# Transposing q and k between the scores of two pairs, and weight conversion behind the first norm, in a fused attention and feed-forward kernel

## The chip, the cores and the metric

The kernel runs on one core of a Trainium2 chip. The metric is the device time of one execution in microseconds (us). All runs quoted here are of the state "fast" (granted TensorE clock 0.996 to 0.999 on average), so they can be compared with each other.

Engine names in the profile: PE is TensorE's matmuls, PEld its weight loads, DVE is VectorE, ACT is ScalarE, POOL is GpSimd, SP is SyncE, which issues most transfers; SPq is its queue. A PSUM bank is one of the buffers that the program's matmuls write to; a tag is the program's name for a group of them.

## The reference, cut to what matters

```python
# attention: q, k, v of shape (8, 12, 448, 64)
q_n, k_n = rmsnorm(q, g_q), rmsnorm(k, g_k)
scores = matmul(q_n, k_n^T) / sqrt(64)
attn = exp(scores - max) / sum(exp(scores - max))
out = matmul(attn, v)
# x: (8 * 448, 768), then a feed-forward block
xn = x / sqrt(mean(x*x) + 1e-6) * rms_g
y = (silu(xn @ w_gate) * (xn @ w_val)) @ w_out      # weights arrive as float64
```

Heads are taken in pairs: 8 batches of 6 pairs make 48. The weights are float64 and must be made float32 on the chip. That is the "conversion": 72 pieces, each in a "turn" that also moves on the pieces before it.

## The kernel before: the parts that the change and the argument touch

One function writes the program, and the traces show VectorE and ScalarE taking their instructions in the order in which that function issues them. In the trace before, ScalarE's L532, which VectorE's copy L533 waits for, ended at 106.71 us (106.10 + 0.61), and the copy ran at 108.79, behind an L748 that was issued ahead of it and started at 107.48. `pe(fn)` issues one piece of TensorE work, and `after(n, fn)` issues something n such pieces later. Two names are alike: `turn(g, i)` transposes q or k of pair g, and `turns(n)` issues n turns of the conversion. One turn of the conversion touches every engine but TensorE:

```python
def convert():                       # turn n; loads, splits, joins and adds of different pieces
    n = turn_of["n"]
    ...
    nc.gpsimd.tensor_tensor(data(key), top, lo, ALU.add)       # L785, GpSimd: piece n-5
    join(...)    # L746, L747, L748, VectorE: piece n-4
    split(...)   # L740, L741, ScalarE: piece n-3
    load_raw()   # L727, SyncE: piece n, into one of 7 raw buffers
    keep(...)    # L773, SyncE: piece n-7 to memory
```

The transposes of q and k. Outside the first pairs (`todo` not empty) both use tag m, which has one bank:

```python
def turn(g, i):                       # i = 0: q, i = 1: k
    ps = (ps_m if todo else ps_f).tile(..., tag="m" if todo else "f")
    for t in range(3):
        nc.tensor.transpose(ps[:, ...], src[:, ...], ident)                    # L527
    if i == 0:
        nc.tensor.transpose(ps[:, 384:], rest, ident)                          # L531
        nc.scalar.activation(qT, ps[:, 0:448], Copy, scale=gqk)                # L532
        nc.vector.tensor_copy(kT[:, LAST], ps[:, 448:])                        # L533
    else:
        nc.vector.tensor_copy(kT[:, FULL], ps[:, FULL])                        # L535
```

The rest of a pair is `score` (L545, six matmuls on four banks of tag s, each followed by an exp on ScalarE, L549), `rests` (L575, L581, L586; the exp is L590), `values` (L597), `sums` (L610, then reciprocal L614 or L618 and multiply L625 on VectorE). L581 starts a product in the bank of tag m and therefore waits for L625 of the pair before (in the trace before, one L625 ends at 43.21 us and the L581 behind it starts at 43.36).

The loop, for the pairs that run alone (1 to 6), for pair 7 with the first norm, and for the stage after, where projections of the feed-forward (L1121) fill the gaps:

```python
for g in range(NG + 1):
    ...
    if g <= NPAIR:                                   # NPAIR = 6
        pe(lambda: score(g, (0,)))
        squares(g + 2, 0); squares(g + 2, 1)
        if g > 1:
            pe(lambda: turn(g + 1, 0)); some_rests(g); pe(lambda: turn(g + 1, 1))
        pe(lambda: rests(g))
        pe(lambda: values(g - 1))
        ...
        turns(1 if g == 1 else 3 if g < NPAIR else 0)      # conversion
        pe(lambda: sums(g - 1))
        pe(lambda: score(g, (1, 2)))
        turns(2 if g == 1 else 3 if g == NPAIR else 0)     # conversion
        continue
    pe(lambda: (rests(g), score(g, (0,)) if g < NG else None))
    if g == NPAIR + 1:
        pe(lambda: rms_x(0))                         # L645, L647, L649
    pe(lambda: values(g - 1))
    if g == NPAIR + 1:
        pe(lambda: score(g, (1,))); pe(lambda: norm_x(0)); pe(lambda: score(g, (2,)))   # L657, L663
    pe(lambda: sums(g - 1))
    if g == NPAIR + 1:
        begin(0, 15)                                 # from here projections lie in todo
    ...
    fill(); squares(...); pe(lambda: turn(g + 1, 0)); some_rests(g); fill()
    pe(lambda: turn(g + 1, 1)); fill()               # every item of a fill is followed by one turn of conversion
```

## Time and profile before

| | before |
|---|---|
| median of 3 runs | 1598.26 us (1598.19 to 1600.19) |
| TensorE busy, of a span of 1596.4 us | 1571.4 us |
| VectorE busy / GpSimd busy | 872.9 / 658.6 us |
| first value product (L597) starts at | 18.98 us |
| feed-forward (L1121) starts at | 97.74 us |
| value products of pair 7 start at | 118.61 us |

First TensorE at the start of the feed-forward (start in us, duration, operation; a wait would stand at the end of a line in brackets):

```profile
104.61 0.49 PE L527 MATMUL tr<-ident,qn 128*128 128x128 f32 x3
104.94 0.27 PE L531 MATMUL tr<-ident,rest 128*128 128x128 f32 x1
105.05 4.68 PE L1121 MATMUL ff<-x,w 128*128 128x448 f32 x12
109.56 0.49 PE L527 MATMUL tr<-ident,qk 128*128 128x128 f32 x3
109.89 6.93 PE L1121 MATMUL ff<-x,w 128*128 128x448 f32 x18
```

And VectorE over the same time:

```profile
101.03 0.62 DVE L625 TENSOR_TENSOR x<-av,rd 128x448 f32<-128x448 f32 x1
101.58 0.35 DVE L746 TENSOR_SCALAR xs<-xs 128x384 f32<-128x384 f32 x1
...
108.79 0.21 DVE L533 COPY kT<-tr 128x64 f32<-128x64 f32 x1
```

The q transposes of pair 8 end near 105.1. Their bank is emptied only when L533 ends at 108.79 + 0.21 = 109.00, because nine steps of three conversion turns (and one step of the first projections, L1131) stand ahead of that copy. The k transposes want the same bank at 109.56. The slack is 0.56 us. No wait is seen, so nothing in the list of waits points here.

### The profile page before, as it was taken

To read this page: it belongs to the slowest core of one execution; us is meant where nothing else is said; L and a number is where in the kernel's file an instruction comes from. 1 tells how busy PE (TensorE), PEld (TensorE's weight loads), DVE (VectorE), ACT (ScalarE), POOL (GpSimd) and SP (SyncE) were. 2 spreads that over 40 slices of the span, in tenths; PEclk is the share of its full clock that TensorE was granted. 3 is DMA by queue.
4 is the path that set the end of the run, shared out by engine and by line. 5 is a ranking of instruction groups with operands and counts; after the bars stand their busy time and mean duration, and the time that the engine had idled before them with its cause. 6 is when DMAs were issued, how large, how long until landed. Compare 5 with 4: busy or idle time off the path is not lost.

```text
span 1596.4 us, 21562 instructions
## 1 busy us (share of the span) xinstructions
PE 1571.4 (98%) x7286; PEld 1113.4 (70%) x7286; DVE 872.9 (55%) x1556; ACT 470.4 (29%) x940; POOL 658.6 (41%) x712
## 2 busy tenths in 40 slices
PE   8999999999999999999999999999999999999998
PEld 4344445687756887578865788667885688859974
DVE  6889898578823556236562354625563355613531
ACT  6745563232222222222232222323322222101010
POOL 6867877465334443343434443443542342000000
PEclk9999999999999999999999999999999999999999
DMA  7648574957746554465545655584554544457651
GB/s 211 205 152 257 162 251 125 289 184 246 247 140 206 151 160 118 143 204 150 157 119 144 205 154 146 152 264 134 159 144 123 179 139 138 120 172 217 175 151 55
DMA packets 261996, 273.28 MB, mean 171 GB/s; under 512 B 78836, under 2 KB 258804, under 8 KB 261876
## 3 DMA queue, kind: packets, MB, share of 16 engines
q1 hardware_dynamic: 260948, 271.61, 56.7%
q8 instruction: 60, 0.98, 0.3%
q14 instruction: 60, 0.49, 0.1%
q10 hardware_dynamic: 800, 0.20, 0.1%
q0 software_dynamic: 128, 0.00, 0.0%
HBM read 232.40 MB, written 39.32 MB: 170 GB/s over the span
## 4 chain that ended last, share of the span: by engine, by line
PE 79%; DVE 7%; issue 1%; POOL 0%; DMA 0%; ACT 0%; SPq 0%; DVEq 0%; POOLq 0%
PE ff L902 40%; PE ff L1093 22%; PE sc L545 6%; PE av L597 5%; PE sc L575 2%; PE den L610 2%; PE tr L527 1%; DVE top L747 1%; DVE top L748 1%; DVE top L746 1%; PE ff L1003 1%; DVE rd L618 1%; DVE h L925 0%; DVE h L924 0%; DVE raw L984 0%
## 5 line engine op out<-in xcount | busy, mean ns | idle before, releaser
L902 PE MATMUL ff<-x,w 128*128 128x224 f32 x1878 | 381.5, 354 | 3.7 <-DVE h L925 2.6
L902 PEld LDWEIGHTS ff<-x,w 128*128 128x128 f32 x1878 | 351.3, 190 | 19.2 <-issue 11.1
L555 POOL TENSOR_TENSOR es<-e 128x448 f32<-128x448 f32 x82 | 91.6, 1137 | 492.8 <-ACT e L549 492.8
L902 PE MATMUL ff<-xs,w 128*128 128x224 f32 x1374 | 281.4, 353 | 2.9 <-DVE w L858 2.9
L902 PEld LDWEIGHTS ff<-xs,w 128*128 128x128 f32 x1374 | 258.1, 190 | 6.3 <-issue 6.0
L562 POOL TENSOR_TENSOR es<-es,e 64x448 f32<-64x448 f32 (+1 forms) x164 | 191.7, 1179 | 6.3
L618 DVE RECIPROCAL rd<-rd 128x448 f32<-128x448 f32 x41 | 121.0, 2952 | 110.8 <-ACT rd L617 110.8
L549 ACT ACTIVATE e<-sc,rs 128x448 f32<-128x448 f32 x288 | 161.6, 635 | 50.4 <-PE sc L545 48.0
L1093 PE MATMUL ff<-w,h 128*128 128x384 f32 x498 | 167.8, 487 | 0.6 <-ACT p L1072 0.6
L1093 PE MATMUL ff<-w,raw 128*128 128x384 f32 x468 | 159.5, 487 | 0.3 <-DVE y L1065 0.3
L545 PE MATMUL sc<-qT,kT 64*128 64x448 f32 x576 | 138.0, 572 | 1.9 <-ACT e L549 0.7
L1093 PEld LDWEIGHTS ff<-w,h 128*128 128x128 f32 x498 | 93.5, 190 | 64.5 <-issue 1.3
L1093 PEld LDWEIGHTS ff<-w,raw 128*128 128x128 f32 x468 | 87.6, 190 | 60.9 <-issue 2.6
L597 PE MATMUL av<-e,vt 128*64 128x448 f32 x576 | 118.8, 548 | 0.0
L506 POOL TENSOR_TENSOR rs<-ms,mhalf 128x12 f32<-128x12 f32 (+1 forms) x50 | 114.4, 2288 | 4.2
L1121 PE MATMUL ff<-x,w 128*128 128x448 f32 x288 | 111.8, 541 | 0.0
L545 PEld LDWEIGHTS sc<-qT,kT 64*128 64x128 f32 x576 | 53.9, 185 | 82.4 <-issue 68.5
L914 DVE TENSOR_TENSOR cc<-ff,u 128x448 f32<-128x448 f32 x84 | 52.4, 624 | 91.6 <-PE ff L902 91.4
L597 PEld LDWEIGHTS av<-e,vt 128*64 128x64 f32 x576 | 37.1, 136 | 75.6 <-issue 75.6
L1121 PEld LDWEIGHTS ff<-x,w 128*128 128x128 f32 x288 | 53.3, 190 | 50.8 <-issue 49.0
L631 POOL TENSOR_TENSOR ss<-ss,rd 128x448 f32<-128x448 f32 x40 | 46.5, 1163 | 82.9 <-ACT rd L630 82.9
L914 DVE TENSOR_TENSOR u<-ff,p 128x448 f32<-128x448 f32 x42 | 26.1, 622 | 96.8 <-PE ff L902 96.8
(132 smaller groups left out, 1855.8 us busy)
## 6 DMA issues: line engine op xcount, KB each, us to landing
w<-kept SPq DMA_DIRECT2D x511, 192.0 KB, 2.7
w<-kept_o SPq DMA_DIRECT2D x296, 192.0 KB, 2.7
kept<-w SPq DMA_DIRECT2D x89, 192.0 KB, 3.8
qk<-in_q_dram SPq DMA_DIRECT2D x48, 192.0 KB, 2.9
qk<-in_k_dram SPq DMA_DIRECT2D x96, 96.0 KB, 3.3
vt<-in_v_dram SPq DMA_DIRECT2D x48, 192.0 KB, 2.5
raw<-in_moe_w_gate_dram SPq DMA_DIRECT2D x24, 384.0 KB, 4.5
raw<-in_moe_w_val_dram SPq DMA_DIRECT2D x24, 384.0 KB, 4.6
```

The source lines that it names most:

```text
L506: nc.gpsimd.tensor_tensor(st["rs", g][:, cols], ms, mhalf[:, cols], ALU.pow)
L545: nc.tensor.matmul(ps[:, 0:S], lhsT=kT[r, c * 128:(c + 1) * 128], rhs=qT[r, :], start=True, stop=True)
L549: nc.scalar.activation(e, ps[:, 0:S], ACT.Exp, scale=rs[:, n:n + 1])
L555: nc.gpsimd.tensor_tensor(es, st["e", g, 0, j], st["e", g, 1, j], ALU.add)
L562: nc.gpsimd.tensor_tensor(es[r], es[r], e[r], ALU.add)
L597: nc.tensor.matmul(av[own(j), 0:S], lhsT=vt[:, j, c], rhs=st["e", g, c, j], start=False, stop=(c == NK - 1), skip_group_check=True)
L618: nc.vector.reciprocal(rd, rd)
L631: after(1 if soon else 4, lambda: (nc.gpsimd.tensor_tensor(ss, ss, rd, ALU.add), st.update({("summed", b): hp})))
L902: nc.tensor.matmul(bank[:, w * HT:(w + 1) * HT], lhsT=wt[:, c * 128:(c + 1) * 128], rhs=x[:, c, :], start=onto is None and w == c == 0, st ...
L914: nc.vector.tensor_tensor(add[name], ps[:, 0:S], add[other], ALU.add)
L1093: nc.tensor.matmul(ps, lhsT=left_o(b, which, LEFT_O[name], c), rhs=data(("wo", b, name, c)), start=first and c == 0, stop=c == NFP - 1, sk ...
L1121: nc.tensor.matmul(bank[w][:, 0:S], lhsT=data(key)[:, c * 128:(c + 1) * 128], rhs=st["x", 0, half][:, c, :], start=half == c == 0, stop=ha ...
```

## The change

Its intent: in the pairs that run alone, TensorE's six scores in a row stall on banks that ScalarE has still to free (0.55 us of each row, by the prediction's estimate from 3.21 us for twelve matmuls, 1.74 for eight and up to 0.95 for four), so the transposes are put between them. In pair 7 a score fills the wait for a bank. And three conversion turns, which stood ahead of the first norm, are moved behind it.

```diff
         if g <= NPAIR:
+            if g > 1:
+                pe(lambda: turn(g + 1, 0))
+                pe(lambda: turn(g + 1, 1))
             pe(lambda: score(g, (0,)))
             squares(g + 2, 0)
             squares(g + 2, 1)
             if g > 1:
-                pe(lambda: turn(g + 1, 0))
                 some_rests(g)
-                pe(lambda: turn(g + 1, 1))
             pe(lambda: rests(g))
 ...
             pe(lambda: score(g, (1, 2)))
-            turns(2 if g == 1 else 3 if g == NPAIR else 0)
+            turns(2 if g == 1 else 0)
 ...
-        pe(lambda: (rests(g), score(g, (0,)) if g < NG else None))
         if g == NPAIR + 1:
+            pe(lambda: score(g, (0,)))
+            pe(lambda: rests(g))
             pe(lambda: rms_x(0))
+        else:
+            pe(lambda: (rests(g), score(g, (0,)) if g < NG else None))
 ...
         if g == NPAIR + 1:
             begin(0, 15)
+            turns(3)
```

## The prediction

> **What bounds the kernel now.** I read the page first, then the table of busy time by stretch, TensorE's timeline of the first 100 us, VectorE's and GpSimd's beside it, and last the chain that ended last. From the page:
>
> ```profile
> span 1596.4 us, 21562 instructions
> PE 1571.4 (98%) x7286; PEld 1113.4 (70%) x7286; DVE 872.9 (55%) x1556; ACT 470.4 (29%) x940; POOL 658.6 (41%) x712
> ...
> PE 79%; DVE 7%; issue 1%; POOL 0%; DMA 0%; ACT 0%; SPq 0%; DVEq 0%; POOLq 0%
> ```
>
> TensorE is busy all but 25 us (1596.4 - 1571.4), yet the chain runs 7% of the span through VectorE. The two meet early: the change only touches pairs 2 to 7, the attention that runs alone before the first feed-forward work. By stretch (us; PE, PEld, DVE, ACT, POOL):
>
> ```profile
> 26.00:36.00 10.00, 10.00 (x55) 4.15 (x55) 9.79 (x15) 8.84 (x19) 6.30 (x10) 1.00 0.58 153
> 36.00:46.00 10.00, 8.29 (x41) 3.27 (x39) 9.71 (x19) 7.95 (x17) 8.35 (x9) 1.00 0.77 233
> ...
> 76.00:86.00 10.00, 8.81 (x50) 2.91 (x44) 5.37 (x7) 4.42 (x10) 4.66 (x5) 1.00 0.71 225
> 86.00:96.00 10.00, 8.97 (x48) 3.71 (x50) 8.01 (x13) 5.79 (x12) 7.92 (x8) 1.00 0.55 152
> ...
> 200.00:250.00 50.00, 48.75 (x172) 24.25 (x169) 47.76 (x69) 28.37 (x59) 40.28 (x38) 1.00 0.70 224
> ```
>
> See that VectorE has 0.2 to 0.3 us free in ten while TensorE idles 1.7 at 36 to 46, and that VectorE is again 96% busy at 200 to 250. TensorE's timeline (start, us; at the end of a line, idle time and what ended it):
>
> ```profile
> 36.56 3.28 PE L545 MATMUL sc<-qT,kT 64*128 64x448 f32 x12
> 39.77 0.55 PE L527 MATMUL tr<-ident,qn 128*128 128x128 f32 x3
> ...
> 43.36 0.97 PE L581 MATMUL av<-e,vr 64*64 64x448 f32 x4 [1.71 <-DVE row L1231]
> ...
> 82.02 1.77 PE L545 MATMUL sc<-qT,kT 64*128 64x448 f32 x8
> 83.76 0.97 PE L575 MATMUL sc<-qT,kT 64*64 64x448 f32 x4
> 85.92 0.97 PE L581 MATMUL av<-e,vr 64*64 64x448 f32 x4 [1.19 <-issue]
> ...
> 93.86 0.60 PE L657 MATMUL rb<-ident,rs 112*128 112x112 f32 x4 [1.03 <-POOL rs L649]
> ```
>
> The releasers named are not the real ones at 43.36 and 85.92. The value product needs the only bank of tag "m", which the multiply L625 of the pair before must free; VectorE's own rows say when:
>
> ```profile
> 39.61 2.95 DVE L614 RECIPROCAL rd<-den 128x448 f32<-128x448 f32 x1
> 42.59 0.62 DVE L625 TENSOR_TENSOR x<-av,rd 128x448 f32<-128x448 f32 x1
> ...
> 94.49 3.64 DVE L663 SCALAR_TENSOR_TENSOR x<-x,rg,rb 128x448 f32<-128x448 f32 x6 [1.79 <-PE rb L657]
> 98.05 2.95 DVE L614 RECIPROCAL rd<-den 128x448 f32<-128x448 f32 x1
> ```
>
> 42.59 + 0.62 = 43.21, then the matmul at 43.36. Likewise L625 ends at 85.8 ahead of 85.92. Last, the chain in order of time: from 198 us it is one row of VectorE conversion steps (L746 to L748) up to the last converted weights, which TensorE takes at 279.31.
>
> ```profile
> 277.32 1.95 POOL w L785 x2
> 279.26 0.04 issue
> 279.31 6.07 PE ff L1003 x18
> ```
>
> [...] at 36 to 43 us VectorE finishes nine conversion steps before the reciprocal. So reordering one engine's work moves everything behind it. [...] L746 takes 0.35 us at 85.74 and 1.31 at 86.99, with GpSimd's 1.51 us add and its weight adds beside it. [...] Here L533 waits for ScalarE's L532 on the same bank (59.8 us in total, 32 times).
>
> **The change part by part.** No instruction is added or removed; the comparison of the instruction streams shows only moves.
>
> (1) In pairs 2 to 6 the eight transposes move ahead of the first scores. Today six score matmuls come in a row and need banks that ScalarE has yet to free: 12 issues take 39.77 - 36.56 = 3.21 us. Eight take 83.76 - 82.02 = 1.74 and four unhindered about 0.86 to 0.95 (97.17 to 98.12), so about 0.55 us of each row is a stall hidden in "busy". The transposes (40.68 - 39.77 = 0.91 us) now cover it. At face value 5 x 0.55 = 2.8 us. But I followed the queues by hand with these durations, and the loop through VectorE closes again. L625 of a pair frees the bank; then ScalarE's square (0.5), and now two exps (1.0) and a square (0.5) stand behind it; then VectorE's two sums (1.0), three conversions (3 x 1.27 = 3.8, somewhat more with GpSimd), reciprocal and multiply (3.6): 10.4 to 11.1 us. Today the mean pair takes (82.02 - 26.11) / 5 = 11.18. So of the 2.8 us only about 0.5 survives: TensorE comes early and waits for L625. A second check eats the rest: q of pair 4 is normed by GpSimd only at 39.2 us, and the transposes would be ready at about 37.7.
>
> (2) Pair 7: its first score now stands before the wait for L625 of pair 5. Idle 1.2 us is filled with 0.95 us of matmul.
>
> (3) The three conversion turns of pair 6 leave the queues ahead of the norm. Today their nine VectorE steps and three GpSimd adds delay the sum of squares (1.51 instead of 1.14 us) and L647, which waits until 92.55. Without them rms follows the add: by hand L647 at 88, root 1.0 us, so the 1.03 us wait at 93.86 goes. Together TensorE begins the feed-forward at about 95.0 instead of 97.74: 0.5 + 0.95 + 1.03 + about 0.2 = 2.7 us earlier.
>
> (4) The price: the nine steps run after the norm and pair 6's reciprocal. VectorE's norm would end at about 95.3, reciprocal and multiply at 98.9, and 3.8 to 6 us of conversion bring it to 102.7 to 105, where before it stood at the same point at 101.58 (98.05 + 2.95 + 0.62). So VectorE, and with it GpSimd's adds, starts the next stage 1 to 3.5 us later, while TensorE starts 2.7 earlier.
>
> (5) From there to 279 us both matter. Today VectorE is held by TensorE at two reciprocals (0.61 at 122.48, 0.51 at 148.27) and GpSimd twice, through ScalarE's tanh, before its sum (0.82 and 0.79); an earlier TensorE gives these 2.7 us back. +1 to +3.5 minus 2.7 is -1.7 to +0.8 at about 200 us. After that the conversion chain has no slack, so its end moves by just that, and TensorE, 2.7 us early, waits at the last output products for it. After 279 TensorE is the bound and the shift stays. The middle of -1.7 to +0.8 is -0.5; I shade it to -1.3, because GpSimd's stretching in (4) is the least sure term and the nine steps may run at their 3.8 us. 1598.26 - 1.3 = about 1597.
>
> **Rivals.** *The whole gain arrives*: TensorE is 98% busy, and if it paces the stage 97 to 279, the 2.7 us (or 5 with all of (1)) reach the end: 1593 to 1595.5. For it: conversion's ScalarE steps stand behind tanhs that wait for TensorE (29.2 us in 12 waits at 96 to 290). Against: VectorE has under 3 us free in 200 to 277. *The conversion slips*: if the nine late steps collide with GpSimd's sums of exps, the ring of four buffers (ScalarE waits 31.9 us for GpSimd's adds there) carries 3 us to the end: 1600 to 1601.5. *The early transposes wait for the norm of q*: pairs gain nothing or lose a few tenths each, TensorE starts at about 96 and the end is 1598 to 1599. A new stall at the single "m" bank in the stage after, where the copy L533 already holds TensorE 0.83 us at 241.20, would look the same.
>
> **Range and chances.** All terms are a few us of 1598, 0.2% each; 2% is 32 us and no path reaches it. The runs before spread by 2.0 us. Prediction 1597.0, range 1594.0 to 1600.0; faster by over 2%: 0.01, within 2%: 0.98, slower: 0.01.
>
> **What would show it.** (1) the row of six scores becomes two rows of 1.7 and 0.9 us with a visible idle before L581 in pairs 3 to 6, ended by L625; pair period 11.0 to 11.2. (2), (3) no wait before the norm's transposes, the first L1121 at 94 to 96 us. (4) VectorE's multiply of pair 6 ends near 99, and the ninth step at 103 to 105. (5) idle of TensorE between 200 and 280 grows from about 2 us to 4 or so, and the first output product after the last conversion starts at 277 to 280. It would be wrong if that product starts by 276, which means TensorE paced the stage, or if the pair period falls below 10.7.

## The result, and the profile after

The changed kernel took 1607.05 us (median of 4; 1606.74 to 1608.88), the kernel before 1598.22 us (median of 4; 1597.96 to 1600.19). The ratio is 1.0055, with a 95% interval of 1.0038 to 1.0072. Ratios here are the mean time of one kernel's fast runs over that of the other's in the same rounds, so not quite the ratio of the medians. The change made the kernel slower by some 9 us: inside 2%, but outside the predicted range and with the wrong sign.

The page after, span, engines and chain:

```profile
span 1605.0 us, 21557 instructions
PE 1572.9 (98%) x7286; PEld 1113.5 (69%) x7286; DVE 873.0 (54%) x1556; ACT 471.0 (29%) x940; POOL 659.5 (41%) x712
...
PE 80%; DVE 5%; POOL 0%; DMA 0%; issue 0%; SPq 0%; ACT 0%; DVEq 0%; POOLq 0%
```

Busy times hardly move. TensorE's idle time grows from 25.0 to 32.1 us (1605.0 - 1572.9), and its busy time by 1.5 us. TensorE's waits name the idle time (total, times, longest):

```profile
PE tr L527 <- DVE kT L533: 7.7, 2, 6.9
...
PE tr L527 <- POOL qn L511: 1.9, 1, 1.9
```

One wait is 6.9 us long. In TensorE's timeline, to be held against the one of before:

```profile
104.44 4.68 PE L1121 MATMUL ff<-x,w 128*128 128x448 f32 x12
116.01 0.90 PE L527 MATMUL tr<-ident,qk 128*128 128x128 f32 x3 [6.90 <-DVE kT L533]
116.71 8.74 PE L1121 MATMUL ff<-x,w 128*128 128x448 f32 x18
```

VectorE after, over the same time:

```profile
100.42 0.62 DVE L625 TENSOR_TENSOR x<-av,rd 128x448 f32<-128x448 f32 x1
100.96 0.35 DVE L746 TENSOR_SCALAR top<-top 128x384 f32<-128x384 f32 x1
...
106.13 0.35 DVE L746 TENSOR_SCALAR xs<-xs 128x384 f32<-128x384 f32 x1
...
108.91 1.28 DVE L746 TENSOR_SCALAR xs<-xs 128x384 f32<-128x384 f32 x1
...
115.75 0.21 DVE L533 COPY kT<-tr 128x64 f32<-128x64 f32 x1
```

The three moved turns occupy VectorE from 100.96 to 106.13, which is 5.2 us. The turns behind them are now stretched too (1.28 us for an L746 that took 0.35). L533 comes at 115.75 instead of 108.79, 7.0 us later: 4.55 because the steps ahead of it start later (106.13 instead of 101.58), 2.41 because these same steps take 9.62 us instead of 7.21. GpSimd was adding beside them (L555, 2.66 us from 107.31); no run separates this stretching from the later place. The slack was 0.56, so TensorE waits.

The wait has a second cost. The table of stretches (busy of PE, PEld, DVE, ACT, POOL; the first number after those is the granted TensorE clock) shows it:

```profile
109.00:116.00 7.00, 0.11 (x1) 0.00 (x0) 6.86 (x9) 0.99 (x2) 5.98 (x6) 0.82 0.77 221
116.00:120.00 4.00, 3.99 (x8) 2.33 (x9) 3.86 (x9) 0.00 (x0) 3.76 (x4) 0.50 0.30 108
```

While TensorE idles, its granted clock falls to 0.50, and the 18 projection matmuls behind the wait take 8.74 us instead of 6.93. By a finer cut of the same table the clock is 1.00 up to about 113.5, 4.4 us into the wait, and at 0.50 until about 120.3, 4.3 us after work began again.

Because the run-up, the stretch ahead of the first value product, varies (last section), I count every kernel's times from its first value product. The 6.90 us of wait, 1.81 us of slow projections and 0.37 us of slow transposes (starts 0.70 instead of 0.33 us apart) are 9.08 us. The value products of pair 7 come 108.38 us after the first instead of 99.63, 8.75 us later, although the feed-forward had started 0.49 us earlier (78.27 instead of 78.76). So 9.24 us were lost between, and 9.08 of them have a name. From there on the distance stays between 8.7 and 8.8 us to the end.

The early pairs did not gain either. TensorE's waits in pairs 3 to 5 after:

```profile
39.80 0.55 PE L527 MATMUL tr<-ident,qn 128*128 128x128 f32 x3 [1.85 <-POOL qn L511]
...
54.64 0.97 PE L581 MATMUL av<-e,vr 64*64 64x448 f32 x4 [0.74 <-DVE kT L533]
...
66.30 0.97 PE L581 MATMUL av<-e,vr 64*64 64x448 f32 x4 [0.80 <-DVE kT L533]
```

Twelve scores in a row took 3.28 us; eight now take 1.77 us and the four behind the transposes 1.02, so most of the stall among them is gone. But the time comes back as a wait for the norm of q and as waits at L581, where the real releaser is again L625 (in pair 4 it ends at 54.49, and L581 starts at 54.64). The reason is the loop that the prediction named, on ScalarE in pair 4, first before, then after:

```profile
50.73 3.26 ACT L549 ACTIVATE e<-sc,rs 128x448 f32<-128x448 f32 x6 [2.61 <-PE sc L545]
53.84 0.97 ACT L484 ACTIVATE sq<-qk 128x384 f32<-128x384 f32 x2
...
55.19 0.61 ACT L630 ACTIVATE rd<-x 128x448 f32<-128x448 f32 x1
```

```profile
54.59 0.58 ACT L630 ACTIVATE rd<-x 128x448 f32<-128x448 f32 x1 [1.44 <-DVE x L625]
55.07 1.14 ACT L549 ACTIVATE e<-sc,rs 128x448 f32<-128x448 f32 x2
56.10 0.93 ACT L484 ACTIVATE sq<-qk 128x384 f32<-128x384 f32 x2
```

The square L630 waits for L625, and the exps and squares that used to run ahead of it now stand behind it. VectorE's sums, and so the next reciprocal, come late. From one pair's value products to the next, from pair 2 up to pair 5, it now takes 11.59, 11.66 and 10.66 us; before, it took 10.45, 11.45 and 10.45. At pair 5 the changed kernel is 1.37 us behind (59.75 against 58.38 after the first value product).

### The profile page after: what moved, and what is told of

The parts are those of the page before. It is cut to its first block, busy times and chain, and to the rows that moved or that the text cites.

```text
span 1605.0 us, 21557 instructions
## 1 busy us (share of the span) xinstructions
PE 1572.9 (98%) x7286; PEld 1113.5 (69%) x7286; DVE 873.0 (54%) x1556; ACT 471.0 (29%) x940; POOL 659.5 (41%) x712
## 4 chain that ended last, share of the span: by engine, by line
PE 80%; DVE 5%; POOL 0%; DMA 0%; issue 0%; SPq 0%; ACT 0%; DVEq 0%; POOLq 0%
PE ff L902 40%; PE ff L1093 22%; PE sc L545 6%; PE av L597 5%; PE sc L575 2%; PE den L610 2%; PE tr L527 1%; PE ff L1003 1%; DVE top L747 1%; DVE top L748 1%; DVE top L746 0%; PE ff L1121 0%; DVE rd L618 0%; DVE h L925 0%; DVE h L924 0%
## 5 line engine op out<-in xcount | busy, mean ns | idle before, releaser
L555 POOL TENSOR_TENSOR es<-e 128x448 f32<-128x448 f32 x82 | 92.1, 1144 | 493.7 <-ACT e L549 493.7
L785 POOL TENSOR_TENSOR w<-top,raw 128x384 int32<-128x384 int32 x63 | 67.0, 1078 | 39.2 <-DVE top L748 25.9
```

Source lines behind the costliest of these rows:

```text
L555: nc.gpsimd.tensor_tensor(es, st["e", g, 0, j], st["e", g, 1, j], ALU.add)
L785: nc.gpsimd.tensor_tensor(data(key).bitcast(I32), top, lo, ALU.add)
```

## The experiments

Theory A: the three turns stand ahead of L533 in VectorE's queue, the one bank of tag m is freed late, TensorE waits and its clock falls. Rival B: the transposes between the scores push the queues late. Rival C: the order of score, last rows and rms in pair 7 does it. Rival D came later: it does not matter where the turns stand, the stage has no room for three more.

All medians of the changed kernels are of 4 runs (5 for the one with the turns behind k in the kernel before, and for the last); those of the kernel before are of 4, 7 or 9 runs on the same chip. "Distance" is counted in one trace of each kernel: the start of the value products of pair 14 after the first ones, minus the 296.63 us of the kernel before.

| kernel | median us | kernel before, same chip | ratio (95%) | feed-forward starts after first value product | distance, us |
|---|---|---|---|---|---|
| before | 1598.2 | | | 78.76 | 0 |
| changed | 1607.05 | 1598.22 | 1.0055 (1.0038 to 1.0072) | 78.27 | +8.74 |
| changed, turns back at pair 6 | 1600.62 | 1598.32 | 1.0017 (1.0000 to 1.0034) | 80.15 | +1.44 |
| before, turns moved alone | 1607.16 | 1598.32 | 1.0053 (1.0036 to 1.0070) | 77.67 | +8.93 |
| before, pairs alone | 1601.25 | 1598.32 | 1.0016 (0.9999 to 1.0033) | 80.13 | +1.41 |
| before, pair 7's order alone | 1599.60 | 1598.32 | 1.0007 (0.9990 to 1.0024) | 78.79 | +0.08 |
| changed, own bank for k of pair 8 | 1605.96 | 1598.25 | 1.0044 (1.0029 to 1.0060) | 78.25 | +6.19 |
| changed, idle matmuls in the wait | 1606.40 | 1598.25 | 1.0051 (1.0035 to 1.0066) | 78.19 | +6.56 |
| changed, turns behind k of pair 8 | 1604.52 | 1598.25 | 1.0037 (1.0022 to 1.0053) | 78.27 | +6.46 |
| before, pair 7's order, turns behind k of pair 8 | 1603.87 | 1598.25 | 1.0033 (1.0019 to 1.0047) | 76.87 | +3.94 |
| changed, turns left to the last burst | 1602.66 | 1599.26 | 1.0024 (1.0009 to 1.0040) | 78.22 | +3.78 |
| before, pair 7's order, one turn each in pairs 9 to 11 | 1603.07 | 1599.26 | 1.0022 (1.0007 to 1.0037) | 76.87 | +4.91 |
| before, pair 7's order, turns ahead of pair 5's sums | 1596.81 | 1599.26 | 0.9990 (0.9977 to 1.0004) | 77.36 | -1.42 |

All gave correct results. The count can be checked: 1598.19 us (the profiled run of the kernel before), plus the distance, plus what the first value product comes later than 18.98 us, gives the time of every other profiled run to 0.15 us (to 0.4 in the one with a turn each in pairs 9 to 11). So the distances tell the kernels apart where the medians, mixed from runs of both run-ups, do not.

### One part undone, each part alone

**The turns back at pair 6.**

```diff
-            turns(2 if g == 1 else 0)
+            turns(2 if g == 1 else 3 if g == NPAIR else 0)
 ...
             begin(0, 15)
-            turns(3)
```

> The changed kernel, but pair 6's three conversion turns stand ahead of the norm again, as before the change. Theory A (the nine VectorE steps that now stand ahead of L533, the copy that frees the one bank of tag m, make the k transposes of pair 8 wait; the granted clock then falls): no wait of over 1 us at those transposes, L533 at 108 to 109 us, the end at 1597 to 1599 us, so all of the 8.6 us come back. Rival B (the transposes between the scores push the queues late): the end stays at 1604 to 1607 us. Rival C (the order of score, last rows and rms in pair 7): stays there too.

The wait is gone and 7.3 of the 8.74 us come back (+1.44). The median lies 1.6 us above the expected range, and L533 came at 110.2 rather than at 108 to 109. I had still taken the pairs for neutral, and they cost 1.4. (Two of its four runs, at 1601.3 and 1601.6, lie 1.4 us or more above the other two, as runs with the slow run-up of the last section do.) Theory A gained on B and C, but not for the whole sum.

**The turns moved alone**, in the kernel before.

```diff
-            turns(2 if g == 1 else 3 if g == NPAIR else 0)
+            turns(2 if g == 1 else 0)
 ...
             begin(0, 15)
+            turns(3)
```

> The kernel before with only the three turns moved behind the norm. Theory A: the same wait, 6 to 8 us, at the k transposes of pair 8 on L533, a granted clock of about 0.8 in the 20 us around it, and the end at 1605 to 1608 us. Rivals B and C: within 2 us of the kernel before, 1596 to 1600 us.

As theory A says:

```profile
117.02 0.90 PE L527 MATMUL tr<-ident,qk 128*128 128x128 f32 x3 [6.92 <-DVE kT L533]
```

The granted clock is 0.74 between 110 and 130 us, and the median 1607.16 us. This part alone makes the whole loss. It also brings what it was meant for: without the turns ahead of it the norm's transposes no longer wait 1.03 us, and the feed-forward starts 1.09 us earlier.

**The pairs alone**: the transposes of pairs 3 to 7 between the scores, in the kernel before (the diff's first hunk).

> The kernel before with only the transposes of pairs 3 to 7 moved between the scores. Theory A: no long wait at the k transposes of pair 8; the pair period stays at 11.0 to 11.5 us because L625 closes the loop, and the end lies within 1.5 us of the kernel before, 1597 to 1600 us. Rival B: 1604 us or more.

No long wait at pair 8, and the trace is 1.41 us behind. By times alone this is unclear (interval 0.9999 to 1.0033), and the median is 1.25 us above the expected range; the profiled run (1601.37) had the slow run-up of the last section, and two others lie beside it. The pairs from 2 on took 11.59, 11.66 and 10.66 us as in the changed kernel, so two of them lie just above the expected 11.0 to 11.5. In the trace this part shows the same waits: 1.82 us for the norm of q, 0.42, 0.74 and 0.80 us at L581. Rival B falls as the cause of the 9 us, but a small loss is its own.

**Pair 7's order alone** (the diff's hunk with `score` ahead of `rests`).

> The kernel before with only pair 7's first score set ahead of its last rows. Theory A: the 1.2 us idle before L581 of pair 7 is filled and the feed-forward starts up to 1 us earlier; the three turns still delay rms, and the end is 1597 to 1599 us. Rival C: 1604 us or more.

The idle 1.19 us before L581 is filled, but the feed-forward starts no earlier: the norm's transposes now wait 1.42 us for the root on GpSimd instead of 1.03, since the three turns still stand ahead of it. Neutral at +0.08. Rival C falls.

### The bank, the clock and the place

**A bank of its own for the k transposes of pair 8.**

```diff
-        ps = (ps_m if todo else ps_f).tile([128, 512], F32, name="tr", tag="m" if todo else "f")
+        if i == 1 and g == NPAIR + 2:
+            ps = ps_s.tile([128, 512], F32, name="tr", tag="s")
+        else:
+            ps = (ps_m if todo else ps_f).tile([128, 512], F32, name="tr", tag="m" if todo else "f")
```

> The changed kernel, all orders kept, but the k transposes of pair 8 write into a bank of tag s, long free, instead of the one of tag m. Theory A1 (the bank alone is the trouble): no wait at those transposes and the end at 1597 to 1599 us. Theory A2 (the late VectorE copies are the trouble wherever they are waited for): L535, the copy of k, still comes at about 119 to 121 us and the scores of pair 8 need it at about 117, so the wait moves there and shrinks from 6.9 to 3 to 5 us; the clock falls less; the end at 1601 to 1604 us.

The transposes no longer wait, and the wait moves, as A2 says (line numbers are 3 higher in this kernel: L548 is the score, L538 the copy of k, L1134 the gate's multiply):

```profile
114.52 4.78 PE L1124 MATMUL ff<-x,w 128*128 128x448 f32 x12 [0.77 <-DVE h L1134]
...
123.09 1.69 PE L548 MATMUL sc<-qT,kT 64*128 64x448 f32 x4 [2.88 <-DVE kT L538]
```

The bank was only the first place where TensorE met VectorE's lateness. The median missed A2's range by 2 us. Its profiled run (1606.28) had a slow run-up, with the first value product at 20.93 us instead of 18.98, which makes up most of it; by distance the kernel is at about 1604.4, just above the range. The clock fell after this shorter wait as well, to 0.50 from 124 to 126 us: four scores took 1.69 us instead of 1.02.

**Idle matmuls in the wait.**

```diff
+            if g == NPAIR + 1:
+                idle_ps = ps_s.tile([128, 512], F32, name="warm", tag="s")
+                for _ in range(25):
+                    nc.tensor.matmul(idle_ps[:, 0:128], lhsT=ident, rhs=ident, start=True, stop=True)
             pe(lambda: turn(g + 1, 1))
```

> The changed kernel with 25 idle matmuls (about 5.8 us of work that nobody reads, into a bank of tag s) ahead of the waiting transposes. Theory A with the clock as a second cost: the copy L533 comes no earlier, so the transposes still start at about 116 us, but TensorE is busy until shortly before, its clock stays at 1.00, the 18 projection matmuls after it take 6.9 instead of 8.7 us, and the end lies 1.5 to 2 us below the changed kernel, at 1604.5 to 1605.5 us. If the clock cost nothing: 1606 to 1608 us; if the wait were not on VectorE but TensorE's own order were too long, 5 us later than the changed kernel, 1612 us.

```profile
108.85 5.75 PE L1354 MATMUL warm<-ident 128*128 128x128 f32 x50
115.95 0.55 PE L527 MATMUL tr<-ident,qk 128*128 128x128 f32 x3 [1.35 <-DVE kT L533]
116.33 6.93 PE L1121 MATMUL ff<-x,w 128*128 128x448 f32 x18
```

TensorE did 5.75 us of useless work and the transposes still started at 115.95, so the wait is VectorE's. The granted clock was 1.00 in every stretch from 109 to 125 us, and the projections behind the wait took 6.93 us again. By distance the clock cost 8.74 - 6.56 = 2.2 us, which agrees with the 1.81 + 0.37 us counted above. The times show it only between runs of like run-up: 1604.55 against 1606.74 us in the two profiled runs, as expected. The median (1606.40) is not within the range; the other three runs lie 2 us higher, as runs with the slow run-up do.

**The turns behind the k transposes of pair 8.**

```diff
             begin(0, 15)
-            turns(3)
 ...
             pe(lambda: turn(g + 1, 1))
+            if g == NPAIR + 1:
+                turns(3)
             fill()
```

> The changed kernel with the three turns of pair 6 issued behind the k transposes of pair 8 instead of ahead of the first projections; nothing else moves. Theory A: L533 at 107.5 to 109 us, L535 near 113 to 114 us, no wait over 1 us, and the end at 1596.5 to 1600 us, perhaps with a small new wait of up to 1 us about pair 9's transposes. Rival (three turns less ahead of the stage cost their 5 us wherever they stand, as VectorE has no room before 279 us): 1603 us or more.

L533 came at 108.39 and the k transposes did not wait, as expected. The end did not follow: 1604.52 us, in the rival's range, so my theory A as a matter of place fell. TensorE now waited at the scores of pair 8 instead:

```profile
125.71 3.87 PE L545 MATMUL sc<-qT,kT 64*128 64x448 f32 x8 [4.28 <-ACT e L590]
```

It waited for banks whose exps stood in ScalarE's queue behind conversion splits (L740):

```profile
119.99 0.56 ACT L740 ACTIVATE top<-raw 128x384 f32<-128x384 f32 x1 [7.51 <-DMA raw<-in_moe_w_gate_dram]
...
124.24 0.55 ACT L740 ACTIVATE top<-raw 128x384 f32<-128x384 f32 x1 [1.69 <-DMA raw<-in_moe_w_val_dram]
...
125.13 0.53 ACT L590 ACTIVATE e<-sc 128x448 f32<-128x448 f32 x1
```

The splits waited for their raw pieces, and the loads had waited for GpSimd's adds to give raw buffers back (SyncE's queue waited 15.8 us in three waits for L785 there; it waited as much before the change, 16.9 us in four, so these waits alone do not make the loss). A turn also issues a load, so three turns put off are three loads put off; that this is what made the splits late was read from the one trace and not tested.

**The same place without the pairs**, in the kernel before, with pair 7's order: the diff is that of pair 7's order and that of the turns above.

> The kernel before, pairs untouched, with pair 7's first score ahead of its last rows and the three turns behind the k transposes of pair 8: the parts of the change that save, without the one that loses 1.4 us in the pairs and without the place that stalls. Theory A: the feed-forward starts 1.1 to 1.6 us earlier than before and this stays to the end: 1596 to 1598 us. Rival (VectorE has no room before 279 us): no gain or a loss, 1599 to 1604 us.

The rival's range came true: the feed-forward started 1.9 us early (76.87), and a wait at pair 8's scores, with a fallen clock (0.91 on average from 110 to 130 us), took it back and more:

```profile
125.23 3.33 PE L545 MATMUL sc<-qT,kT 64*128 64x448 f32 x8 [3.54 <-ACT e L590]
```

So theory A became A': it is not this copy, but any three turns too many in the in-order queues of the stage's first pairs that stalls.

### Is there room in the stage at all?

**The turns given nowhere**: `turns(3)` is taken out of the changed kernel, and the output products of the first block ask for three more turns in one burst.

> The changed kernel with the three turns of pair 6 given nowhere; the twelve output products of the first block then ask for them in one burst before the seventh, at about 270 us. Times are counted from the first value product, at 18.9 us in the kernel before (the run-up before it varies by 1.6 us from run to run). Theory A' (what stalls is any three turns too many in the in-order queues of the stage's first pairs, copy or exp alike): no wait over 1 us from 97 to 260 us, the value products of pair 7 start 98.5 to 99.5 us after the first (99.6 before, 108.4 changed), and the price comes at the burst, 3 to 6 us, so the end is at 1601 to 1605 us. Rival (VectorE has room over the whole stage and only the place was wrong): the burst costs under 1 us and the end is at 1596 to 1599 us.

Both halves of theory A' came true. The value products of pair 7 came 99.10 us after the first, with no long wait before 260 us. The price stood at the burst:

```profile
278.26 0.93 PE L1003 MATMUL ff<-w,h 128*128 128x384 f32 x2 [2.65 <-POOL w L785]
```

With the clock it fell to (0.90 on average from 275 to 280 us, 0.76 from 280 to 285), this makes +3.78 us at the end.

**One turn each in pairs 9, 10 and 11**, in the kernel before with pair 7's order.

```diff
             pe(lambda: turn(g + 1, 1))
+            if NPAIR + 2 <= g <= NPAIR + 4:
+                turns(1)
             fill()
```

> The kernel before with pair 7's first score ahead of its last rows and the three turns of pair 6 given one each to pairs 9, 10 and 11 of the stage, behind their k transposes. Theory A': one turn (1.3 to 2 us of VectorE) per pair fits, because the copy L533 comes 2 us ahead of its use in those pairs; no wait over 1 us there, and what the norm saves stays: 1596.5 to 1598.5 us. If the stage has no room at all for them: 1600 to 1604 us.

A miss: even single turns do not fit. TensorE waited for exps behind conversion splits again:

```profile
177.61 2.48 PE L545 MATMUL sc<-qT,kT 64*128 64x448 f32 x8 [1.73 <-ACT e L590]
206.72 3.01 PE L545 MATMUL sc<-qT,kT 64*128 64x448 f32 x8 [2.60 <-ACT e L590]
```

I had looked for slack on VectorE and found it at L533; the exps on ScalarE had none. What remains is rival D: at the four places that were tried (ahead of the first projections, behind k of pair 8, one each in pairs 9 to 11, in the last burst) the kernels end 3.8 to 8.9 us behind the one before. Four places do not prove that there is no fifth.

**The turns earlier, not later**: ahead of pair 5's sums, where VectorE idled 3.34 us before its reciprocal at 82.20.

```diff
-            turns(1 if g == 1 else 3 if g < NPAIR else 0)
+            turns(1 if g == 1 else 3)
             pe(lambda: sums(g - 1))
             pe(lambda: score(g, (1, 2)))
-            turns(2 if g == 1 else 3 if g == NPAIR else 0)
+            turns(2 if g == 1 else 0)
```

(with pair 7's order of the change)

> The kernel before with pair 7's first score ahead of its last rows and the three turns of pair 6 set EARLIER, ahead of pair 5's sums, where VectorE idles 3.3 us today, instead of behind them. Theory A': the norm is free of them as in the changed kernel and the stage after starts with a lead instead of a debt: reciprocal of pair 5 up to 0.7 us later, feed-forward 0.5 to 1.5 us earlier than before, no wait over 1 us at the k transposes of pair 8, and the end at 1596 to 1598 us, faster than both kernels. If GpSimd's adds then delay the norm of q or the sum of squares instead: 1598 to 1600 us.

```profile
78.59 0.35 DVE L746 TENSOR_SCALAR top<-top 128x384 f32<-128x384 f32 x1
...
81.89 0.74 DVE L748 SCALAR_TENSOR_TENSOR top<-raw,top 128x384 int32<-128x384 int32 x1
82.56 2.94 DVE L614 RECIPROCAL rd<-den 128x448 f32<-128x448 f32 x1
```

The nine steps fit the hole almost to the end: the reciprocal starts 0.36 us later on the clock of the trace. The feed-forward starts 1.40 us earlier by the common count, nothing waits at pair 8, and the lead stays (-1.42 us at pair 14). The median is 1596.81 us (1596.64 to 1598.45), the lowest of all. Against the 9 runs of the kernel before on that chip the ratio is 0.9990 (0.9977 to 1.0004), so by times alone it is not shown to be faster; by one trace of each it is 1.4 us ahead. The times fit that: on that chip both kernels fall into two groups, 1596.6 to 1596.8 and 1598.0 to 1598.5 us here, 1597.9 to 1598.1 and 1599.3 to 1600.0 before, some 1.3 to 1.5 us apart group by group. Which runs belong together was read from the times themselves.

## Why the prediction was wrong, by its own steps

**(1) The pairs.** The mechanism was right and the sum was not. The stall among six scores vanished, the loop through L625 closed and the norm of q was late, all as written; but the pairs lost 1.37 us where 0.5 us of gain was predicted. Two terms were mis-sized. The loop got 10.4 to 11.1 us; it takes 10.66 in one pair, but 11.6 in the two that also square last rows (L448), which stand behind L630 as well. And I held it against a mean pair of 11.18 us, which contains the one slow pair of 13.1 (36.56 to 49.67); an undisturbed pair took 10.45, so the loop was longer than the pair it replaced.

**(2) and (3) Pair 7 and the norm.** Right: no wait before the norm's transposes. From pair 5's value products to the feed-forward the changed kernel takes 18.52 us instead of 20.38, so 1.86 us were saved; 0.95 + 1.03 + 0.2 = 2.2 was the estimate. With the loss in (1) the feed-forward starts 0.49 us earlier, not 2.7, and at 97.13 us instead of at 94 to 96.

**(4) The price on VectorE.** Right in size: the nine steps took 5.2 us, within 3.8 to 6. They ended at 106.2 rather than at 103 to 105, since pair 6's multiply ended at 101.0 and not at 98.9.

**(5) This step failed.** It had the overlap wrong: it let VectorE's lateness travel freely to 279 us and meet TensorE only there, at the last converted weights. It weighed +1 to +3.5 us of debt against 2.7 us that an earlier TensorE would return. The runs showed that the debt is called at once. Some eleven microseconds into the stage the copy L533 had 0.56 us of slack, and it came 7.0 us late; TensorE waited 6.90 us there, and in the kernel with the turns moved alone 6.92. The first output product after the last conversion started at 287.92 us, not between 277 and 280, and TensorE's idle time between 200 and 280 did not grow (1.2 us after, 1.3 before). After it VectorE waited for TensorE in its turn: the reciprocal at 131.10 waited 2.28 us, the same one before 0.61. I had looked for meetings of the two in the list of waits, which shows waits that happened and not those that were missed by half a microsecond.

Of the **rivals**, the last sentence of the third named the very bank and the very copy, but I placed it late in the stage, where the trace before has a wait of 0.83 us, and gave it 1598 to 1599 us. "The conversion slips" was the nearest in time (1600 to 1601.5), with the loss at the wrong end. No rival counted the clock, 2.2 us of the 8.7.

Three **readings** of the trace in the prediction are off, and none of them lies in the step that failed: the row given as 97.17 to 98.12 stands at 197.17 to 198.12; VectorE has 4.77 us free from 200 to 277 (72.23 of 77 us busy), not under 3; and TensorE's idle time there was 1.3 us, not about 2.

What stays open: why single turns in pairs 9 to 11 cost 4.9 us was read in one trace (exps behind splits that waited for GpSimd's adds and for raw pieces) and not tested further. Nor was it tested why the VectorE steps ahead of L533 are stretched, which is 2.41 of its 7.0 us.

## What to carry to other kernels

Before moving work to a later place in an in-order queue, list what stands behind it there and subtract: when does each of those results come, when is it needed, and is the difference larger than the work? A list of waits does not show slack; one has to subtract two rows of two timelines. Work that nobody needs soon belongs in an idle hole ahead (here 3.3 us before a reciprocal), not behind a deadline in a stage whose VectorE is 95% busy (47.76 of 50 us from 200 to 250). And a wait of TensorE should be priced with what the clock takes after it (here 2.2 us after a wait of 6.90).

## The clock and the run-up, as the traces show them

- The clock fell after shorter waits than that of 6.90 us, too. With the bank of its own, after 2.88 us of idleness, four scores took 1.69 us instead of 1.02, and the granted clock was 0.50 from 124 to 126 us. After a wait of 2.65 us (the turns given nowhere) it was 0.76 on average from 280 to 285 us. After one of 2.60 us (one turn each) it was 0.96 on average from 204 to 209 us, and the 18 projections behind the scores took 8.16 us instead of 6.93. Around the one of 1.73 us in the same run it was 1.00 (170 to 180 us).
- The length of the run-up varies, and a kernel's times fall into two groups. In the kernel before and in the pairs alone, ten idle matmuls of the run-up took 1.28 and 2.34 us; the first value products then started at 18.98 and 20.61 us. The times of the kernel before fell around 1598.2 and 1600. The records gave the clock as 1.00 in both (0 to 15 us), so only the durations show it; what sets the length, and that it is what splits the times, was not tested:

```profile
7.17 1.28 PE L1240 MATMUL warm<-ident 128*128 128x128 f32 x10
```

```profile
7.12 2.34 PE L1240 MATMUL warm<-ident 128*128 128x128 f32 x10
```

- Deferred work became a debt at the next deadline behind it in VectorE's queue: 5.2 us of deferred steps, 0.56 us of slack, 6.9 us of TensorE wait.
